# One list of steps for eight batches of attention and mixing: the order of the work, and three pieces of it moved to other engines

## The chip, the cores and the metric

The kernel runs on one core of a Trainium2 chip. The metric is device time in microseconds of one execution. TensorE (PE) multiplies, VectorE (DVE) and ScalarE (ACT) empty its results and do the elementwise work, GpSimd (POOL) does elementwise work on SBUF, and SyncE (SP) issues nearly all transfers. Each engine works through its own instructions in the order in which they were written, and waits on semaphores for the others.

## The reference

Eight batches, eight heads, 576 positions, 64 channels per head. Attention is the sum of a coarse and a narrow one; its output goes through a token mixing and a channel mixing.

```python
q_d, k_d, v_d = (x.reshape(B, H, 144, 4, D).mean(axis=3) for x in (q, k, v))
out_up = np.repeat(sm_attn(q_d, k_d, v_d), 4, axis=2)         # pooled attention, 144 x 144
mask = np.abs(pos[:, None] - pos[None, :]) < 4                # local attention, 7 wide
attn = softmax(np.where(mask, scale * q @ k.T, -1e9))
x = (out_up + attn @ v).transpose(0, 2, 1, 3).reshape(B, S, 512)
h = np.maximum(x.transpose(0, 2, 1) @ w_tok1, 0.0) @ w_tok2   # tokens: 576 -> 256 -> 576
u = x + h.transpose(0, 2, 1)
out = u + np.maximum(u @ w_ch1, 0.0) @ w_ch2                  # channels: 512 -> 1536 -> 512
```

## The kernel before

**A batch.** `load` fetches q and k (four tiles `qk`, one per pair of heads), `load_v` the values of the pooled attention (eight tiles `vr`, added up in fours on POOL into `vd`), `load_w` the windows of v (`vw`). `pool_q` adds q and k up in fours into `qd` on DVE. Then come the pooled attention, `pooled`, once for each of four pairs of heads (scores `sd`, maximum and subtraction on DVE, exponent on ACT, transposes `td`, products `ad`, division into `od`), and the local attention, `local`, once for each of five tiles of positions (scores `sc`, softmax on DVE and ACT, transposes `pT`, products `av`). The pooled result `od` is copied by a transfer into further rows of `vw`, so that the products `av` add both attentions; `av` therefore waits for this copy (`("full", b)`).

`mix` does the token product into `acc` (30 matmuls of 512 columns, in three passes of split operands), its ReLU (`hid`), and eight quarter-halves of the second token product with x transposed on top, which gives `u`. From batch 2 on, `combined` scales u, and splits seven combinations of its blocks (B11, T1, T2, B22, B21, T3, T4) into high and low f16 parts `uh`, with ACT for the high and DVE for the low part.

**The channel mixing.** Batches 0 and 1 use the weights as they are: `first` makes 12 blocks in each of two halves, 12 matmuls of 288 columns each, `second` as many; so 576 matmuls per batch. Meanwhile `weight_sums` forms sums and differences of weight blocks, alternately on POOL and on DVE with ACT, pair after pair (six pairs for the first weights, six for the second), each held back by `after_products` until the products beside it have been issued, and stores them in DRAM as units. Batches 2 to 7 use a scheme with seven products in place of eight: `first_blocks` makes, for each of six pairs of weight blocks, seven products of six matmuls (PSUM tiles X, Y and Z, named `cx`, `cy`, `cz` in the profile), whose sums are formed by ACT and DVE between them, the low parts of T2, T3 and T4 by POOL and of T1 by DVE. `second_blocks` makes seven products of 18 matmuls for each of two output halves (`dX`, `dY`, `dz`), each added into u by DVE; then the output goes out. Weight units are fetched into a ring of six (`wa`, `wb`, `wc`).

**What sets the order.** Steps are written as generators that yield an engine, an assumed duration, what they need, and the PSUM slots that they take and give back. `drive` picks step after step by the earliest assumed start, and writes its instructions at that place. It orders everything up to the end of batch 0 and the scaled u of batch 1. From there on the order is written by hand: for batch 1 and for each later batch the main products are written one after the other, and after each of them `tick` writes as much side work (the next batch's attention, in the sequence of the string `ORDER`, then its mixing, then the load after that) as a share of the time allows. In these loops PSUM tiles of a kind are taken in rotation. PSUM has two double tiles (`gg`: scores, transposes, `av`, `acc`, `u`), three single tiles (`m`: main products), and one (`g`: Z, `ad`, `pT`).

Lines that the steps name: 135 (`mm3`, all three-pass products), 412 (qk load), 441 and 442 (pooling of v), 462 and 464 (pooling of q and k), 476 to 512 (`pooled`), 517 (copy of od into vw), 536 to 577 (`local`), 874 (output of a plain half), 982 (`first_blocks`), 1005 (low parts on DVE), 1009 (low parts on POOL), 1104 (`second_blocks`), 1119 (addition into u).

Of the kernel before, what the change touches and what calls it, by code (L numbers as in the profile page):

```python
# [26 lines left out]
FR = 0.9  # L27
SIDE = 72.0
WEIGHT = dict(P=1.0, V=0.5, A=0.25)
# [3 lines left out]
PATIENCE = 0.15  # L33
DEPTH = 3
PRIORITY = "LpWUMASETaCDPHmQwh"
ORDER = """p0+p1 p0 p1 p0 p1 l0+l1 l0 l1 p0 p0 p1 p1 l0 l1 l0 l1 p0 p0 p1 p1 l0 l0 l1 l1
p2+p3 p2 p3 p2 p3 l2+l3 l2 l3 p2 p2 p3 p3 l2 l3 l2 l3 p2 p2 p3 p3 p3
l0+l4 l0 l2 l2 l4 l4 l4 l1+l2 l1 l2 l3 l3 l4 l4 l3+l4 l3 l4"""
# [3 lines left out]
def tile_ups_attention_mixer(ctx, tc, qk, vw, vr, w1, w2, c1, c2, out):  # L42
# [15 lines left out]
    def open_pool(k, name, side):  # L58
        if k in opened:
# [6 lines left out]
    HOME = dict(cw="B", h="B", SG="B", SV="B", h7="B", f="B", uh0="A", uh1="A", wy="A", ring="A", uh="A", f2="A")  # L66
    psum = ctx.enter_context(tc.tile_pool(name="psum", bufs=1, space=bass.MemoryType.PSUM))
    BUFS = dict(cw=6, h=5, xh=3, x=4, u=6, uh0=4, uh1=4, qk=4, qd=1, vw=1, vd=1, pt=2, od=1, sm=12, ev=8, sc=24,
                SG=3, SV=3, wy=4, ring=6, uh=7, f2=2, h7=6, f=9)

    SLOTS = dict(gg=2, m=3, g=1, w=3)
    now_in = {k: 0 for k in SLOTS}
    driven = [False]

    def slot(k):

        if not driven[0]:
            now_in[k] = (now_in[k] + 1) % SLOTS[k]
        return k + str(now_in[k])

    def T(shape, dt, tag, name):
        if tag == "w":
            return sb.tile(shape, dt, tag=slot(tag), name=name, bufs=1)
        return (pools[HOME[tag]] if tag in HOME else sb).tile(shape, dt, tag=tag, name=name, bufs=BUFS[tag])

# [45 lines left out]
    last_product = [None]  # L131

    def mm3(ps, lhs, rhs, first, last, **kw):
        for i, (a, c) in enumerate(PASSES):
            last_product[0] = nc.tensor.matmul(ps, lhs(a), rhs(c), start=first and i == 0, stop=last and i == 2, **kw)  # L135
# [12 lines left out]
    clock = dict(A=2.0, G=5.0, V=2.0, P=0.0, S=0.0, D=0.0)  # L148
# [5 lines left out]
    def step(engine, us, *needs, at=None, take="", give=""):  # L154
        return engine, us, needs, at, take.split(), give.split()
# [18 lines left out]
    def drive(streams, until):  # L174

        items = [[g, next(g, None), 0.0] for g in streams]
        driven[0] = True
        while not all(u in made for u in until):
            some = []
            for it in items:  # L180
                if it[1] is None or not may(it[1]):
                    continue
                e, us, needs, at, take, give = it[1]
                if any(not free[k.split('>')[0]] for k in take):
# [3 lines left out]
                some.append((t, it))  # L188
            best = min(some, key=lambda x: x[0])
            best = next(x for x in some if x[0] <= best[0] + PATIENCE and (x[0] == best[0] or x[1][1][0] == best[1][1][0]))  # L190
            t, it = best
            e, us, _, _, take, give = it[1]
            if e == "P" and ("uh", 0, 1) not in made and free["g"]:
                keep_busy(min(8, int((t - clock["P"]) * 0.6 / 0.22)))
# [7 lines left out]
            it[2] = t + us + 0.12  # L202
# [7 lines left out]
        driven[0] = False  # L210
        for k, n in SLOTS.items():
            first = min(free[k], key=free[k].get) if free[k] else [i for (x, _), v in held.items() for i in v if x.split(">")[0] == k][0]
            now_in[k] = (first - 1) % n
        return [it for it in items if it[1] is not None]
# [32 lines left out]
    def token_weight(i, n, f):  # L247
        yield step("A", 0.0, ("W", "raw", i))
        raw = made["W", "raw"][i]
        if i < len(TILES):  # L250
            y = WY[i] = T([f.shape[0], n], F32, "SG" if i < 3 else "SV", f"W1_y{i}")
        else:
            y = WY[i]
# [163 lines left out]
    def load_v(st):  # L417
# [4 lines left out]
        def fetch(i):  # L422
            pr, g = divmod(i, 2)

            tag = "w" if st.b > 1 else "x" if st.b or i < 4 else "xh" if i < 7 else "od"
# [19 lines left out]

    def load_w(st):
# [7 lines left out]
    def pool_q(st, hp):  # L454
        e = yield step("V", 1.62, at=st.at[hp])
# [4 lines left out]
        for h in range(2):  # L460
            o = st.qd[:, hp, 0, G * h:G * h + G].rearrange("p (r g) -> p r g", g=HG)
            nc.vector.tensor_reduce(o, q[:, h], axis=AX.X, op=ALU.add)
        k = st.qk[hp][:, S + 3:S + 3 + S].rearrange("p (g f) -> p g f", f=4)
        nc.vector.tensor_reduce(st.qd[:, hp, 1], k, axis=AX.X, op=ALU.add)
        make(("q", st.b, hp), e)

    def pooled(st, pr):
# [3 lines left out]
        yield step("P", 0.65, ("q", b, pr), *([("pair", b, pr - 2)] if pr > 1 else []), take="gg")  # L471
# [8 lines left out]
        yield step("V", 1.68, take="w", give="gg")  # L480
        pd = T([G, 2, 2, Sd], F32, "w", f"pd{b}_{pr}")
        nc.vector.tensor_reduce(mx, s, axis=AX.X, op=ALU.max)
        for par in range(2):
            nc.vector.tensor_tensor(pd[:, par], s[:, par], mx[:, par].unsqueeze(2).to_broadcast([G, 2, Sd]),
                                    ALU.subtract)
        yield step("A", 0.68)
        nc.scalar.activation(pd, pd, AF.Exp, scale=0.125 / 16)
        yield step("P", 0.55, take="gg", give="w")
# [9 lines left out]
        yield step("P", 1.2, ("v", b, 2 * pr + 1), take=one, give="w")  # L498
# [6 lines left out]
        if pr == 0:  # L505
            st.od = T([G, 2, 2, 4, D], F32, "od", f"od{b}")
            st.od_at = st.od.rearrange("p a h r d -> p h a r d")
        r = T([G, 2, 2], F32, "sm", f"rd{b}_{pr}")
# [4 lines left out]
                                ALU.mult)  # L513
        if pr == 3:
# [284 lines left out]
    def ahead(b):  # L799
# [3 lines left out]
        if b > 1:  # L803
            load_w(st)
# [514 lines left out]
```

## Time and profile before

| | us |
|---|---|
| median of three runs | 960.41 (956.75 to 961.88) |
| the profiled execution | 961.94 |
| its span, first to last instruction | 960.2 |
| mean granted TensorE clock | 0.952 |

The page of a profile lists, for each engine, busy time, share of the span and number of instructions. The views by stage give the busy time of each engine in a stretch of time, the clock that TensorE was granted (1.00 is full speed), the mean busy share of the sixteen DMA engines and the bandwidth. A row of a timeline has the start, the time from the first start to the last end of a merged group, the engine, the line, and the tiles (output <- inputs) with their shapes; a bracket at its end tells how long the engine had been idle and whom it waited for. Matmuls are pipelined: a group's duration includes the drain of its last matmul, so what a group costs is read from its start to the start of the next.

### The profile page before, as it was taken

The numbers are of one execution on the slowest core, as the hardware profiler recorded it, in microseconds if no ns is written. First come the engines' busy times: TensorE is split into PE (matmuls) and PEld (weight loads), VectorE is DVE, ScalarE is ACT, GpSimd is POOL, SyncE is SP. The second block draws the span as 40 slices with busy tenths as digits, with TensorE's granted clock in tenths as the row PEclk, the third lists the DMA queues.
The fourth block names the chain that finished last, engine by engine and source line by source line (L and its number), as shares of the span: only waits on it lengthen the run. The fifth ranks groups of instructions, "written<-read, shape, count | busy, mean of one in ns | idle before, by whom it ended". The sixth has DMA issues, their size and how long they took to land. (4 is left out here: it accounts for less than half of the span.)

```text
span 960.2 us, 26341 instructions
## 1 busy us (share of the span) xinstructions
PE 879.6 (92%) x11017; PEld 686.2 (71%) x11021; DVE 654.4 (68%) x1527; ACT 397.5 (41%) x886; POOL 264.6 (28%) x394
## 2 busy tenths in 40 slices
PE   7698997997899899799979999899988999899998
PEld 4466876876777667587757877678766877678776
DVE  7758994466677978736867389654977368644762
ACT  2367542333242356513654156422555136532650
POOL 6241211045756613500134002330134001210230
PEclk9689999898999979899999999799997999999999
DMA  8887247311354524764367343773357542434553
GB/s 242 236 288 243 71 125 191 80 50 57 99 172 114 191 89 145 200 173 155 103 188 198 130 150 115 208 189 130 125 139 212 168 168 89 97 109 132 189 173 123
DMA packets 71015, 145.43 MB, mean 151 GB/s; under 512 B 16720, under 2 KB 32592, under 8 KB 69648
## 3 DMA queue, kind: packets, MB, share of 16 engines
q1 hardware_dynamic: 70576, 143.16, 49.6%
q8 instruction: 86, 1.41, 0.6%
q10 hardware_dynamic: 320, 0.59, 0.3%
q14 instruction: 33, 0.27, 0.1%
HBM read 120.91 MB, written 20.45 MB: 147 GB/s over the span
## 5 line engine op out<-in xcount | busy, mean ns | idle before, releaser
L1009 POOL TENSOR_TENSOR h<-v,h 128x288 f16<-128x288 f32 x36 | 29.5, 818 | 375.8 <-ACT h L1001 360.1
L982 PEld LDWEIGHTS <-wa 128*128 128x128 f16 x864 | 84.6, 99 | 33.7 <-issue 7.3
L1104 PEld LDWEIGHTS <-wc_S 128*128 128x128 f16 x864 | 81.7, 98 | 24.8 <-issue 4.4
L441 POOL TENSOR_TENSOR vr<-vr 72x256 f32<-72x256 f32 x64 | 51.5, 804 | 149.5 <-DMA vr<-in_vr_dram 114.0
L982 PEld LDWEIGHTS <-wb 128*128 128x128 f16 x648 | 61.8, 100 | 32.5 <-issue 15.1
L982 PE MATMUL cx<-uh_T,wb 128*128 128x288 f16 x432 | 69.1, 287 | 11.7 <-DVE y L1028 11.7
L135 PE MATMUL c<-uh,CW 128*128 128x288 f16 x576 | 77.0, 290 | 0.0
L135 PE MATMUL c<-h,CX 128*128 128x288 f16 x576 | 76.2, 288 | 0.0
L1104 PEld LDWEIGHTS <-wc_A 128*128 128x128 f16 x648 | 62.1, 98 | 18.5 <-issue 2.7
L135 PEld LDWEIGHTS <-CW 128*128 128x128 f16 x576 | 55.6, 99 | 16.0 <-issue 1.9
L135 PEld LDWEIGHTS <-CX 128*128 128x128 f16 x576 | 55.2, 99 | 14.8 <-issue 0.5
L1009 POOL TENSOR_TENSOR h<-t,h 128x288 f16<-128x288 f32 x72 | 55.4, 775 | 31.7 <-ACT h L1001 30.9
L572 PE MATMUL av<-vw,pt 47*32 47x64 f32 x2304 | 40.0, 264 | 23.3 <-DMA vw<-od 13.4
L135 PE MATMUL t<-W,hid 128*128 128x288 f32 x336 | 59.0, 309 | 1.0 <-DVE hid L668 0.8
L135 PE MATMUL t<-xh,W 128*128 128x512 f32 x210 | 58.9, 417 | 0.2 <-ACT x L577 0.2
L1104 PE MATMUL dX<-h,wc_S 128*128 128x288 f16 x432 | 57.9, 286 | 0.0
L1104 PE MATMUL dY<-h,wc_S 128*128 128x288 f16 x432 | 57.8, 286 | 0.0
L1104 PE MATMUL dX<-h,wc_A 128*128 128x288 f16 x432 | 57.3, 286 | 0.3 <-DVE u L1119 0.3
L572 PEld LDWEIGHTS av<-vw,pt 47*32 47x32 f32 x2304 | 31.9, 125 | 34.4 <-issue 18.2
L503 PE MATMUL ad<-vd,ptd 72*72 72x65 f32 x512 | 42.6, 241 | 13.8 <-ACT ptd L497 5.5
L1001 ACT ACTIVATE h<-t 128x288 f16<-128x288 f32 x108 | 48.1, 445 | 16.3 <-DVE t L1012 16.0
L1119 DVE SCALAR_TENSOR_TENSOR u<-dX,io,u 128x288 f32<-128x288 f32 x48 | 24.7, 515 | 43.4 <-PE dX L1104 43.4
(195 smaller groups left out, 1898.4 us busy)
## 6 DMA issues: line engine op xcount, KB each, us to landing
qk<-in_qk_dram SPq DMA_DIRECT2D x32, 579.0 KB
wa<-d1a SPq DMA_DIRECT2D x36, 512.0 KB
wc_S<-d_S SPq DMA_DIRECT2D x48, 384.0 KB
wb<-d1b SPq DMA_DIRECT2D x36, 384.0 KB
wc_A<-d_A SPq DMA_DIRECT2D x36, 384.0 KB
vr<-in_vr_dram SPq DMA_DIRECT2D x64, 144.0 KB
C_raw<-in_c_dram SPq DMA_DIRECT2D x16, 512.0 KB
out_dram<-u SPq DMA_DIRECT2D x24, 288.0 KB
```

The source lines that it names most:

```text
L135: last_product[0] = nc.tensor.matmul(ps, lhs(a), rhs(c), start=first and i == 0, stop=last and i == 2, **kw)
L441: nc.gpsimd.tensor_add(t[:, 0:2], t[:, 0:2], t[:, 2:4])
L503: nc.tensor.matmul(ps[:, g, par], pt[:, par, kg, G * g:G * g + G], st.vd[:, kg, 2 * pr + par], start=kg == 0, stop=kg == 1)
L572: nc.tensor.matmul(ps[QB * j:QB * j + QB, par, D * hp:D * hp + D], pt[p, hp, QB * j:QB * j + QB], st.vw[p, g, h, D * hp:D * hp + D], start ...
L982: nc.tensor.matmul(ps, w[:, a, 128 * k:128 * k + 128], uh[x][:, k, c], start=first_ and k == j == 0, stop=k == 1 and j == 2, skip_group_ch ...
L1001: nc.scalar.activation(h[:, PARTS.index(name), 0], x, f, scale=scale)
L1009: eng.tensor_tensor(h[:, i, 1], x, h[:, i, 0], ALU.subtract)
L1104: nc.tensor.matmul(ps, w[:, k, a], H[k][:, i, c], start=first_ and k == j == 0, stop=k == 5 and j == 2, skip_group_check=True)
L1119: nc.vector.scalar_tensor_tensor(u, at[kind], io, u, ALU.mult, ALU.add)
```

## The change

- `drive` now orders all steps of all eight batches; the hand-written loops, `ORDER`, `together`, `tick` and `after_products` go. Steps of the main products of batches 1 to 7 stand last in the list and take PE whenever nothing earlier in the list can start. A step on PE whose kind of tiling differs from the last one's is counted 0.1 us later (`TURN`).
- The work of `first_blocks` and `second_blocks` on ACT, DVE and POOL becomes steps of its own (`after`, `after_second`); their f32 tiles (`f`) and all PSUM tiles are slots that steps take and give.
- Gates: scores of batch b wait for the last first-block product of batch b-2 (`opens`, from batch 4 on); `av` of batch b waits for a product of batch b-1's first blocks (`GATE`).
- u has eight tiles in place of six, and the second token product of batch b waits for the output of batch b-2, not b-1.
- From batch 2 on, q and k are pooled by POOL (three adds each in place of a reduce), and all weight sums are made by POOL, as are the low parts of T1.
- From batch 2 on, the pooled maximum is not subtracted by DVE; it is negated and scaled and goes into the exponent as ACT's bias, in four activations in place of one, which read PSUM.
- The loads of batch b are steps that follow the last scores (qk) and the last `av` (vw) of batch b-1; each weight unit is fetched when the unit six before it has been used.

```diff
+GATE = (0, 0, 1, 2, 3)
+BIASED = range(2, 8)
+HOP = 0.12
+TURN = 0.1
...
-                SG=3, SV=3, wy=4, ring=6, uh=7, f2=2, h7=6, f=9)
-    SLOTS = dict(gg=2, m=3, g=1, w=3)
+    BUFS = dict(cw=6, h=5, xh=3, x=4, u=8, uh0=4, uh1=4, qk=4, qd=1, vw=1, vd=1, pt=2, od=1, sm=12, ev=8, sc=24,
+                SG=6, wy=4, ra=3, rb=3, uh=7, h7=6)
+    SLOTS = dict(gg=2, m=3, g=1, w=3, f=9)
...
+        else:
+            o = st.qd[:, hp, 0].rearrange("p (h r g) -> p h r g", h=2, g=HG)
+            for to, x in ((o, [q[:, :, :, :, f] for f in range(4)]), (st.qd[:, hp, 1], [k[:, :, f] for f in range(4)])):
+                nc.gpsimd.tensor_add(to, x[0], x[1])
+                nc.gpsimd.tensor_add(to, to, x[2])
+                nc.gpsimd.tensor_add(to, to, x[3])
...
+    def opens(b):
+        return [("product", b - 2, 5, "B21")] if b > 3 else []
...
+        if b in BIASED:
+            yield step("V", 0.75)
+            nc.vector.tensor_reduce(mx, s, axis=AX.X, op=ALU.max)
+            nc.vector.tensor_scalar(mx, mx, -0.125 / 16, None, ALU.mult)
+            yield step("A", 1.3, take="w", give="gg")
+            pd = T([G, 2, 2, Sd], F32, "w", f"pd{b}_{pr}")
+            for par in range(2):
+                for g in range(2):
+                    nc.scalar.activation(pd[:, par, g], s[:, par, g], AF.Exp, bias=mx[:, par, g:g + 1], scale=0.125 / 16)
...
-            make(("full", b), e, 3.0 if b else 5.0)
+            make(("full", b), e, 2.5)
...
-        e = yield step("P", 1.08, ("full", b), ("vw", b), take="gg")
+        e = yield step("P", 1.08, ("full", b), ("vw", b), *([("mixed", b - 1)] if b else []),
+                       *([("product", b - 1, GATE[t], "B11")] if b > 2 else []), take="gg", mode="half")
...
-                                   *([("over", b - 1, 0)] if b and (ch == 0 if b < 2 else c == 1) else []), take=f"gg>{b}" if new else "")
+                    before = [("over", b - 2, 1)] if b > 1 else []
...
+    def later(b):
+        every = range(len(TILES))
+        yield step("S", 0.1, *(("sc", b - 1, t) for t in every))
+        st = load(b)
+        make(("loaded", b), now[0])
+        yield step("S", 0.1, *(("av", b - 1, t) for t in every))
+        load_w(st)
...
     def fetch():
+        for k, (shape, src, name) in enumerate(all_units()):
+            yield step("S", 0.1, ("stream",), ("kept", "C2" if name[1] == "c" else "C1"), *([("used", k - 6)] if k > 5 else [("uh", 2, "T4")] if k % 2 else []))
+            unit[k] = T(shape, F16, "rb" if k % 2 else "ra", name)
+            nc.sync.dma_start(unit[k], src)
+            make(("unit", k), fetched(shape[1] * 131072.0, 300e3))
...
+    def reopen():
+        yield step("R", 0.0, ("half",), ("ends", 1), ("kept", "C1"), *(("W", "split", i) for i in range(len(pieces))), ("mixed", 0))
+        open_pool("A", "stream", "right")
+        make(("stream",), now[0])
+        yield step("R", 0.0, ("over", 1, 1), ("kept", "C2"), ("tile", 1, 4))
+        open_pool("B", "hidden", "left")
+        HOME["f"] = "B"
+        make(("hidden",), now[0])
...
+        for b in range(2, B):
+            streams = sum((after(b, n) for n in range(len(FIRSTS))), [lazily(lambda b=b: after_second(b), ("done", b, 0, "A11"))]) + streams
+            ok = ("loaded", b)
+            streams.append(later(b))
+            streams += [lazily(lambda i=i, b=b: mix_of(b)[i], ok) for i in range(4)]
+            pooleds, locals_ = attend(b)
+            streams += pooleds + locals_
+            streams.append(lazily(lambda b=b: pool_all(ready[b]), ok, *(("sd", b - 1, pr) for pr in range(4))))
+            streams += [lazily(lambda g=g, b=b: later_v(ready[b], g), ok) for g in range(2)]
+        if B > 2:
+            late.append(through(*(lazily(lambda b=b, f=f: f(b), ("hidden",), ("uh", b, "B11")) for b in range(2, B) for f in (first_blocks, second_blocks))))
+            streams = [fetch()] + streams + [weight_sums()]
+        drive(streams + late)
```

More of the change, by code (lines that the diff above doesn't have):

```diff
@@ L172, in keep_busy, with drive @@
                 nc.tensor.matmul(ps, junk[:, :128], junk, start=True, stop=True)
-    def drive(streams, until):
+    def drive(streams):
         items = [[g, next(g, None), 0.0] for g in streams]
-        driven[0] = True
-        while not all(u in made for u in until):
+        mode = None
+        while True:
+            items = [it for it in items if it[1] is not None]
+            if not items:
+                break
             some = []
             for it in items:
[L181 to L184, printed above, removed]
+                e, us, needs, at, take, give, m = it[1]
+                if not may(it[1]) or any(not free[k.split('>')[0]] for k in take):
                     continue
@@ L187, in drive @@
                         + [min(free[k.split('>')[0]].values()) for k in take])
-                some.append((t, it))
+                some.append((t + (TURN if e == "P" and m != mode else 0.0), t, it))
+            assert some, [(it[1][0], [n for n in it[1][2] if n not in made], it[1][4]) for it in items]
             best = min(some, key=lambda x: x[0])
[L190 to L194, printed above, removed]
+            t, it = next(x for x in some if x[0] <= best[0] + PATIENCE and (x[0] == best[0] or x[2][1][0] == best[2][1][0]))[1:]
+            e, us, _, _, take, give, m = it[1]
+            if e == "P":
+                if ("uh", 0, 1) not in made and free["g"]:
+                    keep_busy(min(8, int((t - clock["P"]) * 0.6 / 0.22)))
+                mode = m
             now[0] = max(now[0], t)
@@ L209, in drive @@
                 it[1] = None
[L210 to L214, printed above, removed]
     def to_f32(raw, at, y=None, *needs):
@@ L1107, in second_blocks @@
         for o in range(2):
+            at = st.at = {}
+            for i, name in enumerate(SECOND):
+                k = base + len(SECOND) * o + i
+                kind = {"S1": "Y", "S4": "Y", "A12": "Z"}.get(name, "X")
+                new = kind not in at
+                needs = [] if new else [("into", b, o, {"S2": "A11", "S3": "S2", "A22": "S3", "S4": "S1"}[name])]
+                e = yield step("P", 2.21, ("unit", k), *(("h", b, n, OF[name]) for n in range(len(FIRSTS))), *needs,
+                               at=0.0, take="" if not new else f"m>{kind}{b}_{o}z")
+                if new:
+                    at[kind] = PM(f"d{kind}{b}_{o}")[:, :HALF]
+                product(at[kind], unit.pop(k), OF[name], new)
+                blocks_[b, o, name] = at[kind]
+                make(("used", k), e)
+                make(("done", b, o, name), e)
@@ L1190, in tile_ups_attention_mixer @@
         group["Q"] = products[2:]
-        group["h"] = [lazily(lambda: ahead(2), ("x", 1, last))]
-        streams = [x for k in PRIORITY for x in group[k]]
-        left = drive(streams, [("over", 0, 1), ("C1", NF - 1)] + [("uh", 1, 0)] * (B > 1))
-    def rest(items):
-        while items:
-            some = False
-            for it in list(items):
-                if it[1] is None:
-                    items.remove(it)
-                elif may(it[1]):
-                    some = True
-                    yield it[1]
-                    it[1] = next(it[0], None)
-            if items and not some:
-                yield items[0][1]
@@ L1266, in tile_ups_attention_mixer, with first_plain @@
-    while work.next is not None:
-        work.go()
+        streams = [reopen()] + [x for k in PRIORITY for x in group[k]]
+        late = []
+        if B > 1:
+            ok = [("q", 1, 0), ("c2", 0, 1, 3)]
+            banks1 = [], []
+            streams = [lazily(lambda c=c: first_up(ready[1], c), ("c1", 1, c, 0)) for c in range(2)] + streams
+            streams = [lazily(lambda: second_up(ready[1], 0, banks1[0]), ("c2", 1, 0, 0)),
+                       lazily(lambda: second_up(ready[1], 1, banks1[1]), ("c2", 1, 1, 0))] + streams
+            def first_plain():
+                for ch in range(2):
+                    yield from first(ready[1], ch, ["h"] * 4)
+                    if ch:
+                        make(("ends", 1), now[0])
+                    yield from second(ready[1], ch, banks1[ch])
+            late.append(lazily(first_plain, *ok))
```

668 lines of the change are left out of this document (313 added, 355 removed).

## The prediction, made before the changed kernel was run

> **What bounds the kernel now.** I read the page first, then busy time by stage, then PE's instructions in order of time. The page gives the span and the busiest engine:
>
> ```profile
> span 960.2 us, 26341 instructions
> PE 879.6 (92%) x11017; PEld 686.2 (71%) x11021; DVE 654.4 (68%) x1527; ACT 397.5 (41%) x886; POOL 264.6 (28%) x394
> ```
>
> TensorE is the only engine near its limit, so time can be won only where PE stands or runs slowly. By "busy" that is 960.2 - 879.6 = 80.6 us. The Trainium skill, "Perfetto Trace Analysis", section Identifying the Most-Contended Engine, holds matmul busy time to be a poor measure because matmuls overlap; by it the room may be larger than 80.6 us, and the count below agrees. The stages (columns: stretch and its length, then busy time and count of PE, PEld, DVE, ACT, POOL, granted clock, DMA share, GB/s), cut where products of a new kind begin:
>
> ```profile
> 0.00:87.90 87.90, 71.41 (x953) 45.88 (x958) 61.82 (x149) 41.90 (x84) 37.41 (x70) 0.86 0.84 262
> 87.90:206.65 118.75, 113.05 (x1444) 91.79 (x1444) 83.17 (x198) 46.86 (x95) 17.70 (x30) 0.97 0.42 112
> 206.65:329.12 122.47, 112.27 (x1415) 89.69 (x1413) 90.39 (x187) 38.70 (x86) 80.91 (x116) 0.96 0.39 119
> 329.12:894.60 565.48, 521.70 (x6720) 410.87 (x6718) 385.71 (x915) 245.43 (x557) 114.39 (x162) 0.95 0.50 148
> 894.60:956.40 61.80, 61.16 (x494) 47.99 (x491) 32.75 (x80) 24.63 (x65) 14.20 (x18) 1.00 0.52 165
> ```
>
> Call them A (loading, batch 0's attention and mixing), B (batch 0's plain products), C (batch 1's), D (blocks of batches 2 to 6, with the preparation of 3 to 7 beside them) and E (batch 7's blocks, nothing beside them). I count what PE needs when nothing holds it, from start to start. First the chain that ended last, in order of time, then PE's timeline:
>
> ```profile
> 630.89 1.40 PE t L135 x6
> 632.29 2.22 PE dX L1104 x18
> 634.51 1.40 PE t L135 x6
> ...
> 645.72 0.88 PE t L135 x6
> 646.96 0.88 PE t L135 x6
> ```
>
> ```profile
> 895.32 0.90 PE L982 MATMUL cy<-uh_B,wa 128*128 128x288 f16 x6
> ...
> 896.05 0.90 PE L982 MATMUL cz<-uh_B,wb 128*128 128x288 f16 x6
> ```
>
> One tile of the token product takes 1.40 us, one second-block product 2.22, one quarter-half of the token mixing 1.24 (its transposes included), one first-block product 0.73. Attention, from PE's timeline in C:
>
> ```profile
> 208.21 1.20 PE L476 MATMUL sd<-qd 64*72 64x144 f32 x16
> 209.35 3.11 PE L135 MATMUL c<-uh,CW 128*128 128x288 f16 x24
> 212.39 1.38 PE L536 MATMUL sc<-qk 64*32 64x38 f32 x128
> 213.71 3.11 PE L135 MATMUL c<-uh,CW 128*128 128x288 f16 x24
> 216.66 1.17 PE L494 MATMUL td<-ident,pd 72*72 72x72 f32 x16
> 217.66 3.11 PE L135 MATMUL c<-uh,CW 128*128 128x288 f16 x24
> ...
> 248.79 1.20 PE L503 MATMUL ad<-vd,ptd 72*72 72x65 f32 x16
> 249.83 1.64 PE L135 MATMUL c<-h,CX 128*128 128x288 f16 x12
> ...
> 275.59 1.48 PE L572 MATMUL av<-vw,pt 47*32 47x64 f32 x128
> 277.00 0.66 PE L559 MATMUL pT<-ident,P 128*128 128x128 f32 x4
> ```
>
> Two sd take 1.14, two full sc tiles 1.32, two td 1.00, one ad 1.04, two av tiles 1.41. A batch has four pairs and 4.5 full tiles: 2.28 + 2.00 + 4.16 + 2.97 + 3.17, and five pT, which I put at 0.5 each like td: 17.1 us. So one batch from 2 on needs 42 x 0.73 = 30.7 (first blocks), 14 x 2.22 = 31.1 (second), 5 x 1.40 = 7.0, 8 x 1.24 = 9.9, 0.4 for the maximum of u, and 17.1: **96.2 us**. D holds five of them, 481 us, and took 565.5: **84.5 us lost, 17 per batch**. E needs 61.8 and took 61.8: the blocks' own chains lose nothing even with no work beside them. C needs 576 products of 2.22 / 18 = 0.123 (70.8), attention (17.1) and mixing (17.3) of batch 2: 105.2 of 122.5.
>
> **Where D loses.** PE's timeline and its 4-us stretches around batch 3's attention output, and SP's timeline:
>
> ```profile
> 605.83 0.90 PE L982 MATMUL cx<-uh_T,wa 128*128 128x288 f16 x6
> 608.95 0.90 PE L982 MATMUL cx<-uh_T,wb 128*128 128x288 f16 x6 [2.22 <-DVE y L1028]
> ...
> 622.23 0.91 PE L982 MATMUL cz<-uh_B,wb 128*128 128x288 f16 x6
> ```
>
> ```profile
> 608.00:612.00 4.00, 1.51 (x32) 0.93 (x39) 3.12 (x9) 1.23 (x3) 0.00 (x0) 0.72 1.03 228
> ...
> 616.00:620.00 4.00, 4.00 (x120) 3.14 (x101) 3.54 (x10) 3.71 (x11) 1.36 (x2) 0.50 0.51 161
> ```
>
> ```profile
> 605.04 1.83 SPq L412 DMA_DIRECT2D qk<-in_qk_dram x3
> ```
>
> The pooled result (od) is copied into vw while the next batch's qk is loading (DMA share 1.03); the products av wait for it, PE stands, and the granted clock falls to 0.50 and stays there with PE full again. Between the end of the first cx row's issue (605.83 + 0.73) and 622.23, 15.7 us, PE did 23 block matmuls (2.8), all of av (3.2) and two pT (0.9), work worth 6.9: 8.8 us lost in one event, half of a batch's 17. The rest are short waits among the attention pieces, which the hand-written ORDER puts between the first blocks.
>
> **The change, part by part.**
>
> *One list of steps for all batches.* Until about 206 us the old kernel already orders its steps by such a list. Two stretches there:
>
> ```profile
> 96.00:120.00 24.00, 24.00 (x220) 19.29 (x219) 22.79 (x54) 12.52 (x27) 5.93 (x10) 1.00 0.24 71
> 120.00:144.00 24.00, 23.94 (x391) 19.15 (x390) 22.52 (x53) 10.32 (x20) 2.51 (x5) 1.00 0.49 125
> ```
>
> PE is full at full clock while VectorE is at 95%, with attention of batch 1 threaded through: an order fixed ahead of the run can hold on the chip. Scores of batch b may now start when the first blocks of b-2 are through, and av only within the first blocks of b-1 (GATE); so od's copy has most of a second-block stage, over 31 us, to land. Its wait goes. Late next is the VectorE work of the first blocks. With u in eight tiles, mixing no longer waits for the output of the batch before; it falls into the first blocks, where unit loads are fewest. It costs nothing beyond buffers as long as the six weight units in flight stay ahead of PE; if not, see the third rival.
>
> *Work moved to GpSimd*, off VectorE, and the exponent's bias. The groups by line, and single durations (min/median/max ns) of two of the lines:
>
> ```profile
> L462 DVE TENSOR_REDUCE qd<-qk 128x72 f32<-128x288 f32 x64 | 26.4, 442 | 13.5 <-DMA qk<-in_qk_dram 13.4
> ...
> L484 DVE TENSOR_TENSOR pd<-sd,mxd 72x288 f32<-72x288 f32 x64 | 26.2, 447 | 0.7
> ```
>
> ```profile
> L487 ACT ACTIVATE pd<-pd 72x576 f32<-72x576 f32 x32 | 21.9, 683 | 31.0 <-DVE pd L484 30.9
> ```
>
> ```profile
> L442 POOL TENSOR_TENSOR vd<-vr x64: 449/458/976, 11.1 to 758.4; 72x128 f32<-72x128 f32 x64
> ```
>
> ```profile
> L1005 DVE SCALAR_TENSOR_TENSOR h<-s,h x36: 446/451/982, 348.4 to 925.3; 128x288 f16<-128x288 f32 x36
> ...
> L1005 DVE SCALAR_TENSOR_TENSOR h<-cx,h x36: 442/448/450, 354.9 to 927.5; 128x288 f16<-128x288 f32 x36
> ```
>
> ```profile
> L1009 POOL TENSOR_TENSOR h<-t,h x72: 723/732/1192, 354.5 to 928.5; 128x288 f16<-128x288 f32 x72
> ```
>
> Per batch VectorE sheds 8 x 0.44 = 3.5 (q; k's reduces come on top), 8 x 0.45 = 3.6 (subtractions) and 6 x 0.45 (T1's low part). It is not the bound in D (385.7 of 565.5), so this buys only shorter waits; I count it at nothing by itself. ScalarE makes 16 exponents of 72x144 of four of 72x576: between no more than 4 x 0.68 and 16 x 0.68 = 10.9 us; I take 5, and ACT at 245 of 565 hides either. (A multiplication of 72x4 per pair comes on VectorE, less than one of the two subtractions that go.) GpSimd gains 24 adds of 128x144: 0.46 (the row's median) to 0.98 (its longest), 11 to 24 us, and six low parts of 0.73. With its 114.4 / 5 = 23 it comes to 38 to 51 of some 100: not the bound, either. The weight sums go to GpSimd wholly: it was busy 80.9 in C with half of them, so at most 162 with all, spread over B and C (its 17.7 in B leaves 100 free there). Their stores of 64 and 128 KB, issued by SP, move with them into B, beside a DMA share of 0.42.
>
> *What that costs.* h<-s,h reads two operands from SBUF and lasts up to 982 ns where its median is 451; h<-cx,h takes one from PSUM and never exceeds 450; GpSimd's own add stretches to 1192. Both slow down when they meet. The Trainium skill, "GPSIMD Engine Reference", section 1 (Specifications), says the same against this change: the SBUF interfaces are shared with VectorE, and its instructions with two SBUF inputs contend. By rows: per batch 62 instructions of some 300 elements (0.45) and five of 512 (0.8, scaled) read two SBUF operands, 32 us; met by GpSimd 38 to 51% of the time it grows by 12 to 16 us, where it grew by some 7 before. What reaches PE lies between 0 (E, 61.8 of 61.8 with both engines at work) and the growth of 9. I take 3.5 per batch, nearer E's row. In B, GpSimd was idle while VectorE ran at 95%; there I take 2.5 lost, between 0 and the 19 us of two-operand work on the second weights (24 of 512 elements).
>
> **The sum**, on the profiled execution's 961.94: D 565.5 -> 481 + 5 x 3.5 = 498.5 (-67); C 122.5 -> 105.2 + 3.8 = 109 (-13.5); B +2.5; A, E and the 3.8 behind the last product unchanged. 961.94 - 78 = 883.9. The median of the runs, 960.41, lies 1.5 below the profiled one: **883 us**.
>
> **Rivals.**
>
> *The output's wait stays* (0.15): od lands late in the new order as well, since qk of the next batch is still issued on the same queue near it. One event of 8.8 per batch: 883 + 5 x 8.8 = 927. For it: share 1.03 above. Against: the gate leaves 30 us.
>
> *The shared port decides* (0.12): GpSimd's new work stretches VectorE to the point where PE waits for it. First blocks with av, token product and mixing need 30.7 + 3.2 + 7.0 + 9.9 = 51 of PE; VectorE has some 36 there (60 x 0.45 for the blocks, 9 for mixing), of which 17 are two-operand: 53 if all double. With 19 instead of 2.5 in B and 5 more per batch: 883 + 16.5 + 25 = 924.
>
> *The transfer queue holds up the units* (0.07, the slower side). SP issues in order, and an entry that waits holds those behind it:
>
> ```profile
> 153.71 4.41 SPq L874 DMA_DIRECT2D out_dram<-u x2
> ```
>
> Out, od, qk, vw and the weight units all stand in this queue in a fixed order now. In the second blocks one unit is used per 2.22 us and six are buffered, 13.3 us ahead. A hold of 13.3 + x costs PE x, and some 4 at half clock. Slower by 0.5% needs (965 - 883) / 5 = 16.4 per batch, so it decides from one hold of 13.3 + 12.4 = 26 us in each; at 30 us it gives 883 + 5 x 20.7 = 986. Against it: the longest wait in front of such a transfer that I found is this 4.4.
>
> *Nothing is won* (0.05): the gates and buffers lead to the old order in effect; 960.
>
> **How the numbers follow.** Forecast 0.61, nearly all within 866 to 905; below 866 (0.05 of it) only if nearly all losses vanish: with none in C and D, and B as now, it would be 961.94 - 84.5 - 17.3 - 1.5 = 858.6. The range 866 to 930 takes in the first two rivals' times and leaves out that 0.05, the last two rivals (0.12) and a little of the first two. A measurement tells about 0.5% (5 us) from no change. Faster by over 0.5%: 0.61 + 0.15 + 0.12, so 0.88; within: 0.05; slower: 0.07.
>
> **What would show it.** Right: no wait of av for vw; granted clock 1.00 from about 180 us on; the first cx near 315 us and 100 us from batch to batch; VectorE's total near 570, GpSimd's near 430. Wrong: PE idle before av with a DMA as releaser (first rival); two-operand VectorE lines with means over 0.6 us and PE waiting for them (second); PE waiting for wc or wb (third); a B longer by over 10 us.

## The result and the profile after

The changed kernel takes **927.99 us** (median of 4 runs, 924.61 to 928.98) against 961.14 before on the same chip (4 runs, 956.75 to 962.39): ratio 0.9657, 95% interval 0.9617 to 0.9697. It is faster, inside the range on record, but it wins 33 us where 77 were forecast.

From the page of the changed kernel: the span, the engines and the granted clock by slices.

```profile
span 926.7 us, 26502 instructions
...
PE 858.6 (93%) x11020; PEld 679.7 (73%) x11024; DVE 617.0 (67%) x1347; ACT 410.5 (44%) x958; POOL 463.2 (50%) x676
...
PEclk9889999899899999999999999999999999999999
```

The same stages as in the prediction, cut at the same events (stretch and length, then busy time and count of PE, PEld, DVE, ACT, POOL, granted clock, DMA share, GB/s):

```profile
89.18:214.48 125.30, 116.25 (x1468) 93.16 (x1467) 88.13 (x187) 48.46 (x95) 107.40 (x149) 0.96 0.44 123
214.48:346.52 132.04, 122.29 (x1791) 100.19 (x1790) 70.33 (x161) 46.38 (x108) 96.20 (x143) 0.96 0.37 100
346.52:859.95 513.43, 489.74 (x6316) 394.62 (x6313) 360.95 (x777) 249.43 (x606) 199.70 (x283) 0.99 0.53 164
859.95:923.00 63.05, 62.41 (x506) 49.19 (x503) 34.38 (x76) 24.67 (x66) 17.51 (x24) 1.00 0.52 167
```

D went from 565.5 to 513.4, and the clock there from 0.95 to 0.99. B and C became longer, 118.8 to 125.3 and 122.5 to 132.0. The list has moved part of batch 3's attention from D into C; the counts of PE's groups in D show how much (five batches would have 160 sd, 320 ad, 1440 sc, 160 td and 100 pT, as before):

```profile
L127 PE MATMUL t<-xh,W 128*128 128x512 f32 x150 | 45.4, 429 | 11.5 <-DVE xh L648 8.7 <-ACT xh L646 2.7
...
L533 PE MATMUL ad<-vd,ptd 72*72 72x65 f32 x256 | 19.6, 231 | 0.0
L607 PE MATMUL av<-vw,pt 47*32 47x64 f32 x1440 | 19.5, 224 | 2.2 <-issue 2.2
...
L569 PE MATMUL sc<-qk 64*32 64x38 f32 x1184 | 14.8, 204 | 0.0
L593 PE MATMUL pT<-ident,P 128*128 128x128 f32 (+1 forms) x92 | 13.5, 268 | 0.0
L523 PE MATMUL td<-ident,pd 72*72 72x72 f32 x128 | 10.8, 227 | 4.9 <-ACT pd L507 4.9
L495 PE MATMUL sd<-qd 64*72 64x144 f32 x128 | 10.5, 293 | 0.0
```

At the prediction's prices the missing pieces (32 sd, 64 ad, 256 sc, 32 td, 8 pT) are worth 2.3 + 4.2 + 2.6 + 2.0 + 1.0 = 12.1 us. D therefore needs 481 - 12.1 = 468.9 and lost 44.5, **8.9 a batch** (before 17). C needs 12.1 more than the 105.2 of the prediction, less 1.1 because 16 sd of batch 2 now run in B: 116.2, and it lost 15.8. B is 6.5 us longer, 5.4 without these sd.

What PE spent in D, kind by kind: each row of PE's timeline is given the time from its start to the next row's start, and these are added up (us; "counted" is the prediction's dense price; q on VectorE and no v sums are experiments below):

```
                  counted   before   after   q on VectorE   no v sums
first blocks        153.3    196.3   165.7          170.5       163.5
second blocks       155.4    157.0   159.3          155.5       155.5
token product        35.0     39.1    50.1           41.0        38.8
mixing               51.6     51.9    52.6           52.0        52.0
attention            73.4    121.4    86.0           80.9        80.4
 (before: counted    85.5, since batch 3's is whole there)
```

The first blocks won 31 us, and attention lost 36 above its count before and 13 after. The wait of av for the od copy is gone from D: its row above has 2.2 us of idle time behind the issue alone. **Given back** is the token product: 11 us more than before, with 11.4 us of waits for xh (x split into a high and a low part, which this product reads). The same two rows in D before:

```profile
L135 PE MATMUL t<-xh,W 128*128 128x512 f32 x150 | 41.8, 412 | 0.0
...
L572 PE MATMUL av<-vw,pt 47*32 47x64 f32 x1440 | 26.4, 274 | 12.5 <-DMA vw<-od 8.4 <-ACT x L577 3.4 <-issue 0.7
```

Two groups of VectorE, before (first fence) and after (second): h<-y,h with two SBUF operands, and h<-cx,h, which takes one operand from PSUM. Both make low parts of the first blocks' results. Columns: count, busy us, mean ns, idle before:

```profile
L1005 DVE SCALAR_TENSOR_TENSOR h<-y,h 128x288 f16<-128x288 f32 x36 | 18.0, 499 | 0.0
...
L1005 DVE SCALAR_TENSOR_TENSOR h<-cx,h 128x288 f16<-128x288 f32 x36 | 16.1, 447 | 0.0
```

```profile
L1053 DVE SCALAR_TENSOR_TENSOR h<-y,h 128x288 f16<-128x288 f32 x36 | 25.3, 702 | 0.3 <-ACT h L1049 0.2
...
L1053 DVE SCALAR_TENSOR_TENSOR h<-cx,h 128x288 f16<-128x288 f32 x36 | 16.1, 446 | 0.0
```

The first grew by 0.20 us in the mean, with GpSimd busy more than before (200 us of D in place of 114); the other, which reads PSUM, did not grow. The timelines of VectorE, GpSimd and TensorE around one wait of 2.5 us:

```profile
696.76 0.97 DVE L1064 SCALAR_TENSOR_TENSOR t<-y,t 128x288 f32<-128x288 f32 x1 [1.44 <-POOL h L1060]
...
699.46 1.21 DVE L648 TENSOR_TENSOR xh<-x_last,xh 128x512 fp32r<-128x512 f32 x1
```

```profile
687.68 0.66 POOL L477 TENSOR_TENSOR qd<-qk 128x144 f32<-128x144 f32 x1
...
695.47 0.57 POOL L479 TENSOR_TENSOR qd<-qd,qk 128x144 f32<-128x144 f32 x1
695.99 1.43 POOL L1060 TENSOR_TENSOR h<-t,h 128x288 f16<-128x288 f32 x2
```

```profile
700.72 1.43 PE L127 MATMUL t<-xh,W 128*128 128x512 f32 x5 [2.52 <-DVE xh L648]
```

From 687.7 to 696.0 GpSimd pools q and k, twelve additions without a gap. The low parts that it makes for the first blocks (h<-t,h) stand behind that in its queue; VectorE waits 1.44 us for them, then runs its next four instructions at 0.97 to 1.21 us beside GpSimd, and xh, the last of them, is late for the token product. Queue and slower instructions both act here; experiments 1 and 8 tell them apart.

In C one event stands out. PE, VectorE and SP's queue:

```profile
251.17 0.39 PE L607 MATMUL av<-vw,pt 47*32 47x64 f32 x2 [7.93 <-DMA vw<-od]
253.04 2.03 PE L607 MATMUL av<-vw,pt 47*32 47x64 f32 x126 [1.48 <-DMA vw<-od]
```

```profile
239.26 0.42 DVE L543 TENSOR_TENSOR od<-ad,rd 72x256 f32<-72x256 f32 x1
```

```profile
241.18 2.99 SPq L902 DMA_DIRECT2D d_A<-CX  x6
245.29 0.81 SPq L902 DMA_DIRECT2D d_S<-S  x2
246.19 1.56 SPq L549 DMA_DIRECT2D vw<-od  x2
```

Batch 2's od is ready at 239.7 and its copy is issued 6.5 us later, behind stores of weight sums. PE stands for 7.9 + 1.5 = 9.4 us. The stretches of 5 us around its return:

```profile
249.00:254.00 5.00, 1.35 (x74) 1.17 (x78) 0.00 (x0) 0.00 (x0) 4.48 (x8) 0.50 0.42 75
254.00:259.00 5.00, 5.00 (x94) 3.69 (x80) 1.80 (x2) 2.89 (x6) 4.66 (x6) 0.54 0.35 87
```

In the second PE is full again, at a granted clock of 0.54.

### The profile page after: what moved, and what is told of

Same layout as the page of the kernel before. It is cut to its first block, busy times and chain, and to the rows that moved or that the text cites. A ratio compares the mean times of both kernels' runs of the same rounds, so it can differ in the third digit from the quotient of the medians.

```text
span 926.7 us, 26502 instructions
## 1 busy us (share of the span) xinstructions
PE 858.6 (93%) x11020; PEld 679.7 (73%) x11024; DVE 617.0 (67%) x1347; ACT 410.5 (44%) x958; POOL 463.2 (50%) x676
## 5 line engine op out<-in xcount | busy, mean ns | idle before, releaser
L1060 POOL TENSOR_TENSOR h<-t,h 128x288 f16<-128x288 f32 x108 | 83.2, 776 | 185.8 <-ACT h L1049 175.9
L987 PEld LDWEIGHTS <-wa 128*128 128x128 f16 x864 | 81.9, 98 | 30.0 <-issue 7.8
L1148 PEld LDWEIGHTS <-wc_S 128*128 128x128 f16 x864 | 84.2, 99 | 22.0
L477 POOL TENSOR_TENSOR qd<-qk 128x144 f32<-128x144 f32 x48 | 30.9, 644 | 76.0 <-DMA qk<-in_qk_dram 76.0
L987 PE MATMUL cx<-uh_T,wb 128*128 128x288 f16 x432 | 64.8, 286 | 1.1 <-DVE y L1091 1.1
L607 PE MATMUL av<-vw,pt 47*32 47x64 f32 x2304 | 34.5, 241 | 25.0 <-DMA vw<-od 14.5
L127 PEld LDWEIGHTS t<-xh,W 128*128 128x128 f32 x210 | 38.1, 192 | 23.4 <-DVE xh L648 12.0
L607 PEld LDWEIGHTS av<-vw,pt 47*32 47x32 f32 x2304 | 28.1, 113 | 34.3 <-issue 24.0
L770 ACT ACTIVATE uh_T<-T,us 128x288 f16<-128x288 f32 x48 | 23.8, 529 | 59.5 <-DVE T L784 59.5
L648 DVE TENSOR_TENSOR xh<-x,xh 128x512 fp32r<-128x512 f32 x28 | 21.5, 774 | 41.0 <-ACT xh L646 40.9
```

What stands on the lines that cost most here:

```text
L477: nc.gpsimd.tensor_add(to, x[0], x[1])
L607: nc.tensor.matmul(ps[QB * j:QB * j + QB, par, D * hp:D * hp + D], pt[p, hp, QB * j:QB * j + QB], st.vw[p, g, h, D * hp:D * hp + D], start ...
L648: nc.vector.tensor_tensor(xh[:, 1], xf(t), xh[:, 0].bitcast(F32), ALU.subtract)
L770: nc.scalar.activation(t[:, k, 0], block[name][k], AF.Copy, scale=s)
L987: nc.tensor.matmul(ps, w[:, a, 128 * k:128 * k + 128], uh[x][:, k, c], start=first_ and k == j == 0, stop=k == 1 and j == 2, skip_group_ch ...
L1060: nc.gpsimd.tensor_tensor(h[:, i, 1], getattr(here(), x), h[:, i, 0], ALU.subtract)
```

## The experiments

Each ran in three rounds beside the kernel before on the same chip; ratios are to that kernel and carry their 95% interval. The changed kernel stands at 0.9657. Where an edit changes a step's engine, assumed time or conditions, the list is ordered anew, so more than that step can move; in 2 and 8 the steps stay as they are.

**1. Pooling of q and k back on VectorE.**

```diff
-        wide = st.b < 2
+        wide = True
```

> As the changed kernel (928 us), but q and k of all batches are added up by VectorE's reduces, with the scheduler told so. Port-and-queue theory (GpSimd's new work in the first blocks delays the low parts that free tiles, and stretches VectorE's two-operand instructions, so xh is late and PE waits): the waits of the token product for xh (8.7 + 2.7 us in all) mostly go, GpSimd's busy time falls by some 85 us, 915 to 922 us. Rival (VectorE is the scarce engine in the first blocks, so relieving it paid): VectorE gains some 37 us and the time rises to 932 to 940.

Measured: 916.87 us, ratio 0.9521 (0.9484 to 0.9559). D, and two of PE's groups in it:

```profile
346.53:846.05 499.52, 483.99 (x6316) 392.25 (x6313) 373.83 (x825) 253.22 (x606) 133.81 (x187) 1.00 0.57 168
```

```profile
L127 PE MATMUL t<-xh,W 128*128 128x512 f32 x150 | 42.7, 415 | 3.0 <-DVE xh L648 2.0 <-ACT xh L646 0.9
...
L987 PE MATMUL cx<-uh_B,wa 128*128 128x288 f16 x181 | 27.6, 288 | 6.1 <-DVE h L1053 6.0
```

D is 13.9 us shorter, and the waits for xh fall from 11.4 to 2.9. VectorE has 13 us more work in D and delivers earlier: moving pooling to GpSimd cost time. The queue shows in this and the stretch does not: VectorE's waits for GpSimd in D fall from 9.1 us to 3.0, while its two-operand groups of the first blocks and xh (h<-y,h, h<-s,h, u<-y,u, t<-y,t, t<-s,u and both xh) together take no less than in the changed kernel, 120.4 us against 119.7. The new waits of cx for h (6.0) show what comes next.

**2. The od copies issued by ScalarE instead of SP** (batches 2 to 7).

```diff
-                (nc.scalar if b < 2 else nc.sync).dma_start(
+                nc.scalar.dma_start(
```

> As the changed kernel, but the copies of od into vw of batches 2 to 7 are issued by ScalarE instead of SP; the order of all other instructions is the same. Queue theory (batch 2's copy stood 6.5 us behind the stores of the weight sums on SP, which wait for GpSimd): PE's 7.9 us wait before batch 2's first av shrinks to 1 to 2, together with the half clock after it 7 to 11 us are won: 917 to 921 us. Rival (the copy's landing under load is what takes long, wherever it is issued): 926 to 930 us.

Measured: 940.62 us, ratio 0.9766 (0.9706 to 0.9825); slower than the changed kernel, which neither side expected. The first block of batch 2 starts at 361.8 us in place of 346.5. ScalarE and PE in C:

```profile
256.39 1.43 ACTq L549 DMA_DIRECT2D vw<-od  x2
257.86 1.02 ACT L849 ACTIVATE h<-c 128x288 f16<-128x288 f32 x3 [17.84 <-DMA d_A<-CX]
```

```profile
261.39 0.39 PE L607 MATMUL av<-vw,pt 47*32 47x64 f32 x2 [17.09 <-DMA vw<-od]
```

od is ready at 240.75 (VectorE's timeline), yet the copy goes out at 256.39, and the releaser of ScalarE's wait is a store of weights on the other queue. So the copy still came after a store that stands ahead of it in the program, though another engine issued it; now ScalarE's own work waits as well. Why a copy waits for a store that it shares no data with, these records don't say.

**3. The maximum subtracted on VectorE again, one exponent for four.**

```diff
-BIASED = range(2, 8)
+BIASED = ()
```

> As the changed kernel, but no batch uses the bias: VectorE subtracts the pooled maximum and one exponent follows, as before. If the bias helps: VectorE gains 18 us over the batches, 930 to 936 us. If its four exponents on ScalarE cost more than VectorE's subtractions (PE's waits of the transposes td for the exponent, about 1.15 us once in most batches, are new): 920 to 925 us. If neither: within 3 us of 928.

Measured: 921.91 us, ratio 0.9576 (0.9521 to 0.9632). The waits of td for pd (4.9 in D) are gone, those for xh stay (11.9). So the bias cost some 6 us, though the interval overlaps that of the changed kernel.

**4. Both 1 and 3.**

> Pooling of q and k back on VectorE and the pooled maximum subtracted on VectorE again, everything else as changed. Theory: the two losses are separate (queue on GpSimd ahead of the splits: 11.1 us; sixteen small exponents on ScalarE ahead of td: 6.1 us) and add up: 928.0 - 17.2 = 910.8, so 908 to 914. Rival: VectorE now has back all the work that was taken off it, and its order delays xh and h in turn; 915 to 922.

Measured: 916.59 us, ratio 0.9530 (0.9496 to 0.9565), the same as 1 alone (0.9521). The two don't add up: with pooling off GpSimd the bias costs nothing that can be measured. The theory of two separate losses fell.

**5. The scheduler told longer times for the weight sums.**

```diff
-            yield step("G", 0.5)
+            yield step("G", 0.65)
...
-                yield step("G", 0.75)
+                yield step("G", 0.9)
```

> Only the durations that the list scheduler assumes for GpSimd's weight sums are raised (0.75 to 0.9, 0.5 to 0.65, 1.2 to 1.9, 1.3 to 1.35 us); the instructions are the same. Theory: batch 1's plain products lose about 9 us because stores of sums that come late stand ahead of batch 2's od copies in program order; with longer assumed times more of these stores come behind the copies, the wait of av for vw<-od (7.9 + 1.5 us, with half clock behind it) goes, and the time is 915 to 920. Rival: the order is not at fault, GpSimd simply has too much to do there; the wait stays or moves, 925 to 931.

Measured: 944.63 us (934.14 to 949.40), ratio 0.9784 (0.9719 to 0.9849), slower than either side had it. The wait of av in C shrinks to 1.5 + 1.5 us and C to 126.9, though B grows to 129.0, and the last stores now end after the first block of batch 2 has begun. ScalarE there, and PE:

```profile
359.77 0.40 ACT L1070 COPY s<-cx 128x288 f32<-128x288 f32 x1 [9.95 <-DMA d_S<-S]
```

```profile
360.22 1.60 PE L987 MATMUL cx<-uh_T,wa 128*128 128x288 f16 x6 [9.74 <-ACT s L1070]
```

Batch 2's blocks take 116.7 us in place of 102.6. The wait behind the stores was named rightly, but this is no remedy: they hold up something else.

**6. The sums' arithmetic left out.** GpSimd computes none; slices of the weights are stored, as many stores as before.

```diff
-                yield step("G", 1.3, ("t1", 0, len(TILES) - 1), (C.name, f), (C.name, f + 2))
+                yield step("S", 0.1, ("t1", 0, len(TILES) - 1), (C.name, f), (C.name, f + 2))
...
-                eng.tensor_tensor(t, a21, a22, add)
...
+                for name, x in (..., ("S1", a21), ("S2", a21), ("S4", a12), ("S3", a22)):
+                    keep(C, p, name, x)
```

> GpSimd's arithmetic of the weight sums is left out: slices of the weights are stored in place of the sums, as many bytes and as many stores, so the output is another. Theory: the sums cost in the two stages of plain products (125.3 and 132.0 us) by late stores ahead of the od copies (about 12 us) and by VectorE's two-operand instructions that stretch beside GpSimd (some 4 us); 908 to 917, no wait of av for vw<-od. Rival: VectorE's order and the work threaded in cost this, not the sums; 923 to 931.

Measured: 957.20 us, ratio 0.9936 (0.9902 to 0.9971); both sides missed, by 26 us and more. SP's queue in B, GpSimd and PE:

```profile
133.87 4.05 SPq L902 DMA_DIRECT2D d_S<-CX  x8
137.97 3.04 SPq L902 DMA_DIRECT2D d_A<-CX  x6
141.04 5.22 SPq L902 DMA_DIRECT2D d_S<-CX  x8
146.37 0.38 SPq L417 DMA_DIRECT2D vr<-in_vr_dram  x1
```

```profile
148.90 0.93 POOL L431 TENSOR_TENSOR vr<-vr 72x256 f32<-72x256 f32 x1 [28.01 <-DMA vr<-in_vr_dram]
```

```profile
167.05 1.95 PE L533 MATMUL ad<-vd,ptd 72*72 72x65 f32 x14 [15.96 <-POOL vd L432]
```

Without GpSimd's steps between them the stores come out back to back, each 0.5 to 0.65 us of SP's time, and batch 1's loads of v stand behind them. B takes 156.0 us. (The stores have as many bytes, but in smaller pieces: the run has 80229 DMA packets, the changed kernel 71015.) This doesn't price the sums; it shows the third rival of the prediction (a transfer queue in fixed order that holds up loads) at work, with other transfers.

**7. The copy of batch 2's od told to land later** (on top of 1): its av products get a later place.

```diff
-            make(("full", b), e, 2.5)
+            make(("full", b), e, 12.0 if b == 2 else 2.5)
```

> Pooling of q and k on VectorE, and the list is told that the od copy of batch 2 takes 12 us to land in place of 2.5, so that its av products come later among batch 1's plain products. Theory: PE's 7.9 + 1.5 us before av and the half clock behind it were all that the late od copy cost, and it goes: 916.7 - 11 = 906, so 904 to 909, batch 1's stage 119 to 123 us in place of 131. Rival: the wait moves (mixing of batch 2 comes later, its pieces stand closer before the first blocks): 913 to 918.

Measured: **906.30 us**, ratio 0.9451 (0.9420 to 0.9481), as the theory had it, and the fastest kernel here that computes everything. C:

```profile
215.35:338.18 122.83, 119.83 (x1792) 98.59 (x1791) 74.85 (x173) 46.46 (x108) 71.06 (x103) 1.00 0.38 100
```

C took 131.9 us in 1 alone (214.62 to 346.53): 9.1 us less, all that the two profiled runs differ by (915.05 to 906.04); by the ratios it is 6.7. That one event made more than half of C's loss of 15.8.

**8. Sums of v left out on GpSimd** (on top of 1; one copy in their place).

```diff
-            nc.gpsimd.tensor_add(t[:, 0:2], t[:, 0:2], t[:, 2:4])
-            nc.gpsimd.tensor_add(st.vd[...], t[:, 0]..., t[:, 1]...)
+            nc.gpsimd.tensor_copy(st.vd[...], t[:, 0]...)
```

> Pooling of q and k on VectorE, and of batches 2 to 7 the two additions that sum v on GpSimd are left out (one copy in their place, so the output is another); GpSimd's work in the blocks falls from 27 to about 18 us a batch, and nothing else. Theory of the shared port: what is still lost there (499 us against 467 counted) comes from VectorE and GpSimd slowing each other; a third less GpSimd work gives a third of it back, 9 to 11 us: 905 to 909. Rival: it comes from the fixed order (products that follow their own chains of VectorE and ScalarE with attention between): 913 to 918.

Measured: 900.18 us, ratio 0.9375 (0.9349 to 0.9400), below both ranges. D, VectorE and PE:

```profile
344.57:834.51 489.94, 481.33 (x6316) 391.52 (x6314) 356.81 (x825) 252.62 (x606) 105.59 (x155) 1.00 0.57 172
```

```profile
L1051 DVE SCALAR_TENSOR_TENSOR h<-y,h 128x288 f16<-128x288 f32 x36 | 20.4, 566 | 0.3 <-ACT h L1047 0.2
```

```profile
L985 PE MATMUL cx<-uh_B,wa 128*128 128x288 f16 x181 | 27.2, 286 | 1.2 <-DVE h L1051 1.0
```

D is 9.6 us shorter than in 1 at the same VectorE instructions (x825); VectorE's busy time falls from 373.8 to 356.8 and h<-y,h from 0.72 (its mean in 1) to 0.57. The groups added up under 1 take 103.8 us in D in place of 120.4, while VectorE's waits for GpSimd stay (2.7 us, in 1 3.0), so here it is not the queue: GpSimd's two-operand work stretches VectorE's, and that reaches PE, whose wait of cx for h falls from 6.0 to 1.0. The whole fell by more, 0.0146 in the ratio, some 14 us; the profiled runs differ by 11.6, with 2.0 ahead of D, and the rest is not explained.

**9. Sums of v on VectorE** (on top of 7): one reduction for two additions.

```diff
-            nc.gpsimd.tensor_add(t[:, 0:2], t[:, 0:2], t[:, 2:4])
-            nc.gpsimd.tensor_add(st.vd[...], t[:, 0]..., t[:, 1]...)
+            nc.vector.tensor_reduce(st.vd[...], t..., axis=AX.X, op=ALU.add)
```

> The kernel with q and k pooled on VectorE and the output of batch 2 planned later (906.3 us), and now the sum of v of batches 2 to 7 as one reduction on VectorE (72x512 to 72x128, one operand) in place of two additions of two operands on GpSimd. Theory of the shared port: what VectorE's two-operand instructions win by having GpSimd out of the way (9.6 us where the sums were left out) outweighs the eight reductions a batch that VectorE has more (8 x 0.5 to 0.7 us, in stretches where it is 77% busy); 897 to 904. Rival: work that comes back to VectorE costs there what it costs on GpSimd, the leaving out counted, not the place: 905 to 911.

Measured: 907.72 us, ratio 0.9455 (0.9407 to 0.9504): no difference from 7. Two of its VectorE groups:

```profile
L448 DVE TENSOR_REDUCE vd<-vr 72x128 f32<-72x512 f32 x48 | 50.0, 1052 | 7.5 <-DMA vr<-in_vr_dram 7.5
...
L1051 DVE SCALAR_TENSOR_TENSOR h<-y,h 128x288 f16<-128x288 f32 x36 | 19.9, 553 | 0.3 <-ACT h L1047 0.2
```

The two-operand instructions do get faster, and PE's wait of cx for h in D falls from 7.5 us (in 7) to 0.4. But the reduction took 1.05 us where 0.5 to 0.7 were expected, 8.4 us of VectorE a batch, and av waits for the od copy again, 2.4 us twice in D. D is as long as in 7 (499.3 us against 498.7). The rival holds for the time; which of the two took the gain back is not shown.

**10. No gate before av** (on the changed kernel).

```diff
-                       *([("product", b - 1, GATE[t], "B11")] if b > 2 else []), take="gg", mode="half")
+                       take="gg", mode="half")
```

> The condition that holds the output products av until a given first-block product of the batch before is taken out; everything else as changed. Theory: the gate is what gives the copy of od time to land; without it PE comes to av too early, waits for vw<-od in each batch as before the change (8.8 us an event, five of them), 940 to 972. Rival: a list order over all batches suffices by itself, the gate is not needed; 923 to 931.

Measured: 922.37 us, ratio 0.9592 (0.9564 to 0.9621). Not slower, against the theory: PE does wait for od again (3.1 + 1.4 us at 322, and some 1.2 us four times in D), but a list order alone keeps most of the time for the copy. The output of batch 3 moves into C.

**11 and 12. No gate, on top of 1 and on top of 9.**

> Pooling of q and k on VectorE and no gate before av. Theory: the two are separate, 11.1 and 5.6 us: 928.0 - 16.7 = 911.3, so 909 to 914. Rival: without the gate av and mixing only pulled work ahead, away from where GpSimd held the splits up; with that gone it gives nothing: 915 to 920.

> The kernel of the run before, without the gate ahead of av. Theory: as without the v sums' move (916.9 to 913.5), a further 2 to 4 us: 894 to 902. Rival: the late od copy of batch 2 was part of what the gate's removal had mended; then no difference from the run before, within 1.5 us.

Measured: 913.53 us, ratio 0.9514 (0.9499 to 0.9528), against 0.9521 for 1; and 912.34 us, ratio 0.9501 (0.9461 to 0.9541), against 0.9455 for 9. The first time lies in the theory's range, but by the ratios the gain is only 0.7 us; the second is outside what either side had. With pooling off GpSimd the gate's removal wins nothing that can be measured.

**13. u in six tiles**, with mixing waiting for the output of the batch before, as it did before the change.

```diff
-x=4, u=8,
+x=4, u=6,
...
-before = [("over", b - 2, 1)] if b > 1 else []
+before = [("over", b - 1, 0)] if b > 1 and c % 2 else [("over", b - 2, 1)] if b > 1 else []
```

> u in six tiles again, with mixing of a batch waiting for the output of the batch before as it did before the change (odd columns of the second token product); everything else as changed. Theory: two more tiles are what lets mixing go beside the first blocks; without them it falls into the second blocks and PE has less to fill the first blocks with: 4 to 8 us a batch over five batches, 945 to 965. Rival: mixing fits in either place, the list order finds room: 926 to 934.

Measured: 947.65 us, ratio 0.9860 (0.9816 to 0.9904). The token product in D:

```profile
L127 PE MATMUL t<-xh,W 128*128 128x512 f32 x150 | 47.3, 441 | 19.3 <-DVE xh L648 19.3
```

Without the two tiles, and with the earlier condition that goes with six, 20 us are lost, more than half of the change's gain. Then the token product's waits for xh are 19.3 in place of 11.4, D takes 523.5 us, and batch 7's first blocks 38.1 in place of 31.9.

## Why the prediction was right in sign and wrong in size

The profiled runs differ by 961.94 - 928.45 = 33.5 us where the sum gave 78. The 44.5 missing, by the prediction's own terms:

- **D, "I take 3.5 per batch, nearer E's row": the step that failed.** It measured 8.9, which makes 27 us of the miss. The bounds held (0 to 9), the choice between them did not. E's row could not carry it: there GpSimd does only low parts (14.2 us of work in 61.8), no pooling and no sums of v, and PE has no token product that waits for xh. And the term priced only the stretch of VectorE's instructions; the busy shares (38 to 51% of a batch) hid that pooling comes as one unbroken run ahead of the low parts, for which there was no term at all. By the runs, pooling on GpSimd is 13.9 us of D's 44.5, with the queue and not the stretch to be seen in it (1), and the sums of v, which were on GpSimd before the change too, are 9.6 more, by stretch (8). Some 21 remain, with the first blocks 10 above their count; these runs don't split that part into port and order.
- **C, "105.2 + 3.8".** It lost 15.8, which makes 12 us of the miss. The wait of av for the od copy, which the prediction took to be gone, came back once, for batch 2, behind the stores of weight sums; told a later landing, it went (7). The prediction had moved these stores "into B" beside a free DMA share and had not followed them through SP's queue.
- **B, 2.5 lost** became 5.4, or 3 us of the miss: GpSimd is busy 107 of 125 us there, against 18 before. Up to 150 us, where VectorE is 92 to 99% busy in both kernels, PE idles 2.8 us there in place of 0.1; a stop of PE around 160 us stood there before too and has more half clock behind it now. What port contention alone costs there wasn't measured: a version that shares the sums between GpSimd and VectorE needs a pool of 41.5 KB per partition where 39.9 were left, so there is no time for it. A and E are 1.3 us longer each.
- **Right: the list itself.** The waits of av for od are gone from D, the granted clock there is 0.99, and the first blocks won 31 us. u in eight tiles, to which the prediction gave no gain of its own, carries 20 us of the 33 (13). The gate, named as what gives the copy its time, isn't needed for it (10).
- **"8.8 us lost in one event, half of a batch's 17"** was put down to the od copy, and that reading was too large. Of it the wait for od was 1.5 us (the row below); 2.2 us were a wait for VectorE's y, as the prediction's own fence shows, 0.7 one for ScalarE's x, and from 612 to 620 the clock was 0.50, some 4 us by estimate. In all of D before, av idled 8.4 us behind that copy. So D's gain, 31 us in the first blocks and 23 in attention, is more than the end of this one wait.

```profile
611.73 1.17 PE L572 MATMUL av<-vw,pt 47*32 47x64 f32 x62 [1.53 <-DMA vw<-od]
```

- **ScalarE's exponents** were said to hide behind a ScalarE at 245 of 565 us. Busy time hides no latency: td waited 4.9 us for them in D, though with pooling off GpSimd the loss vanishes (4).
- **The rivals.** "The shared port decides" came near in time (924), in part by luck: its 5 more per batch in D came out (8.9 against 8.5), of its 16.5 more in B only 3 did, and the loss in C, which it did not name, made up for that. Its place was right (VectorE beside GpSimd), with a queue added that it did not name. The Trainium skill, "GPSIMD Engine Reference", section 1 (Specifications), warned of that contention, and this trace agrees: 0.50 to 0.70 us for two SBUF operands, 0.45 unchanged with one from PSUM. "The transfer queue holds up the units" occurred in another form: late stores held up the od copy in the changed kernel, and the loads of v in experiment 6.
- Of the signs to watch, "two-operand lines with means over 0.6" and PE behind them came true, and "the first cx near 315" fell: it is at 346.5, 12.1 of the difference being batch 3's attention that the list put ahead of it. VectorE's total is 617 us where 570 was expected, GpSimd's 463 where 430 was.

## What to carry to other kernels

Before work is moved to an idle engine, look at what stands behind it in that engine's queue at that moment, and not at the engine's mean share: twelve additions in one run, 8.3 us, delayed what the critical engine needed next. Where an order is fixed ahead of the run, follow each store to the copies and loads behind it in the same order; telling the scheduler one later landing time was worth 7 to 9 us here. Two changes that each help alone may be answers to the same wait, so run them together before their gains are added.

## What the runs showed of the hardware

- After a stop of PE of 9.4 us the granted clock was 0.54 over 5 us in which PE was full again, and after a shorter one (2.8 + 0.9 us, in C of experiment 6) 0.50 over the next 5 us. At these clocks 2.3 and 2.5 of the 5 us are lost on top of the stop, by estimate.

```profile
309.00:314.00 5.00, 5.00 (x29) 4.98 (x29) 0.75 (x3) 1.18 (x4) 2.31 (x4) 0.50 0.25 64
```

- A copy moved to another engine's queue (experiment 2) still went out only at 256.39, 15.6 us after its data was ready, and the wait on that engine ended with a store on SP's queue. The records don't tell whether the chip or the program's semaphores kept that order.
- A reduction of 72x512 to 72x128 on VectorE took 1.02 to 1.08 us in all 48 cases of experiment 9, whether GpSimd was idle or busy beside it, where VectorE's h<-y,h in the same run took 0.44 to 0.99. So it is not GpSimd that makes it long.
